# New instruction orders for an attention kernel's eight pairs, split score products in the first pair, and identity products as filler

## The chip, the cores and the metric

The kernel runs on one core of a Trainium2 chip. A core has five engines that run side by side, each through its own queue in order: TensorE (PE in the profile, its weight loads PEld), VectorE (DVE), ScalarE (ACT), GpSimd (POOL) and SyncE (SP), which here only issues transfers. They meet through semaphores. The metric is the time of one execution on the device in microseconds (us); lower is better. Of the kernel before there are three timed runs and one profiled execution.

## The reference, cut to what matters

```python
# attention: q, k, v are (2, 8, 768, 64) in float32, centroids (8, 16, 64)
q_assign = argmax(einsum(q_n, c_n), -1)         # q_n, k_n, c_n: rows divided by their norms
k_assign = argmax(einsum(k_n, c_n), -1)
mask = q_assign[:, :, :, None] == k_assign[:, :, None, :]
scores = where(mask, (1 / sqrt(D)) * q @ k.T, -1e9)
attn = softmax(scores)
x = (attn @ v) laid out as (1536, 512)
# two layers on 1536 tokens, widths 512 -> 2048 -> 512
h = x @ w1_in;  g = h * cos(h);                              x = g @ w1_out
h = x @ w2_in;  g = h, 0 or (h + 1)**2 / 4, by the size of h;  out = g @ w2_out
```

Every query attends to the keys whose nearest centroid is the same as its own. The cluster test is folded into the score product as extra rows: a second product with few contraction rows adds zero where the clusters agree and a huge negative number where they don't.

## The kernel before, in words

The attention part works on eight pairs of heads (two batches, four pairs of heads each). Each pair has twelve score tiles of 128 queries by 768 keys, `S0` to `S11`; `S0` to `S5` are its first head. A tile is four products on TensorE, two for each half of the keys: one of 128 contraction rows (line 635), and one of 96 rows in the first pair, 80 in the others, which adds the low parts and the clusters (line 638). Then VectorE takes the row maxima (line 645, called max here) and ScalarE the exponential with its row sum (line 653, called Exp here). Two score tiles fit into PSUM at a time, so tile n+2 can begin on TensorE only after Exp of tile n.

Of the first head the exponentials are turned by TensorE (`G`, three 128x128 transpositions into one bank, line 696, which ScalarE copies out, line 698) and multiplied by v (`V`, line 703); VectorE scales the sum by the softmax denominators (`X`, line 713). Of the second head VectorE turns the tile in squares of 32 (`T`, line 741) and TensorE multiplies small blocks of 32 rows (`W`, four steps, line 757); `Z` (lines 769 and 770) adds the partial sums up. `R` is the reciprocal of the row sums (ScalarE line 660, VectorE 661 and 663), `B` spreads it through DRAM. Each pair's q and k are prepared during the pair before: `L` loads, `Q0` to `Q3` turn (line 544) and are copied out, `D`, `C`, `m`, `t`, `n`, `O` find the clusters, `H` and `J` copy the rows into place by DMA.

The order of all this is written out by hand. For each pair a string of words is read from left to right (`run_cycle`), and each word emits its instructions on all engines at once: `BEGIN` for the first pair, `FIRST` for the second, `CYCLE` for the next four, `LATE` and `LAST` for the last two. A prime on a word means the pair before. Nothing is rearranged later, so each engine runs its share in just this order. `w` is one step of converting the layers' weights (mostly one VectorE instruction), `h` one early product of the first layer, `g0` the first of its cosines.

The first pair is prepared by `first_pair`, which ends with its first three tiles. While nothing else is ready there, `run_idle` multiplies a tile of zeros (line 345): `NIDLE` says how many at each of five places. `centroid_setup` loads the exponential's table on ScalarE ahead of need, by an `Exp` whose two result columns go into the tile that takes q of the second pair; so that load waits for it. The two score banks share PSUM with a pool `ps_q` that the preparation uses and closes.

After the eight pairs come the two layers: 2304 products of 128x512 on TensorE, with the element-wise work on the other engines.

Of the kernel before, what the change touches and what calls it, by code (L numbers as in the profile page):

```python
# [9 lines left out]
F32 = mybir.dt.float32  # L10
# [23 lines left out]
NIDLE = (9, 3, 2, 4, 2)  # L34
# [3 lines left out]
def attention_moe_moe(  # L38
# [214 lines left out]
    with ExitStack() as actx:  # L253
# [6 lines left out]
        idle = ap.tile([P, HS], F32, tag="pt", bufs=PT_BUFS, name="idle").bitcast(BF16)[:, :512]  # L260
# [52 lines left out]
        def centroid_setup(ct):  # L313
# [7 lines left out]
            nc.scalar.activation(nat[1][0][:, 0, 0, 0:2],  # L321
# [17 lines left out]
        def first_pair():  # L339
# [9 lines left out]
            run_idle(NIDLE[0])  # L349
# [140 lines left out]
            times(1, nc.gpsimd)  # L490
            one = Prep(1)
# [4 lines left out]
            run_idle(NIDLE[4])  # L496
# [5 lines left out]
            ps_q.close()  # L502
            ps_s.append(actx.enter_context(tc.tile_pool(name="ps_s", bufs=2, space=PSUM, reuse_waits="tile")))
            scores_of(0)
            one.turn(3)
            scores_of(1)
# [118 lines left out]
        def scores(n, step):  # L625

            d, j = divmod(n, NJ)
            i, h = divmod(d, 2)
            qt, kt = prepped[i][h]
            if step == 0:  # L630
                ptile[n] = ps_s[0].tile([P, 2, 512], F32, tag="s", name=f"s{n}")
            s = ptile[n]
            cols = slice(j * P, (j + 1) * P)
            kc = slice(step * HS, (step + 1) * HS)
            nc.tensor.matmul(s[:, step, :HS], qt[:, 0, cols], kt[:, 0, kc],  # L635
                             start=True, stop=False)
            rows = D + C if i else D + 2 * C
            nc.tensor.matmul(s[:, step, :HS], qt[:rows, 1, cols], kt[:rows, 1, kc],  # L638
                             start=False, stop=True)
# [160 lines left out]
        def run_cycle(c, order):  # L800
# [4 lines left out]
            for word in words:  # L805
# [8 lines left out]
                if not 0 <= i < NP and what not in "wIAqhg":  # L814
# [250 lines left out]
```

## Time and profile before

| what | value |
|---|---|
| timed runs | 757.41, 758.57, 761.39 us, median 758.57 |
| profiled execution | 758.55 us; its span from first to last instruction is 756.6 us |
| TensorE busy | 744.2 us of the span (98%) |
| VectorE busy | 593.4 us (78%) |
| ScalarE busy | 372.5 us (49%) |
| GpSimd busy | 266.8 us (35%) |
| mean granted TensorE clock | 0.998 |

The span is what the trace covers; the 1.95 us between the span and the time of that execution lie around it. Matmuls overlap in their pipelines, so a busy TensorE may still run slower than its best; distances from one start to the next show that better than busy time. "Idle before" in a row is the engine's idle time right ahead of it, and the arrow names what ended it. The granted clock is 1.00 at 2.4 GHz and 0.50 at 1.2 GHz.

### The profile page before, as it was taken

Reading aid. Unit: us, or ns where it says so; the run is one execution under the profiler, and the core shown is the slowest. Engines: PE = TensorE matmul, PEld = TensorE weight load, DVE = VectorE, ACT = ScalarE, POOL = GpSimd, SP = SyncE. Lnnn points to the kernel's source line nnn. Section 1 sums busy time; section 2 is a strip of 40 time slices with the busy share of each in tenths; the row PEclk is TensorE's granted clock in tenths of the full one; section 3 lists DMA queues with packets and bytes.
Section 4 is the critical chain, followed back from the end, with each engine's and each line's share of the span. In section 5 each row is a group of like instructions: output and inputs, shape, how many; then the busy total and the mean of one; then the engine's idle time right before and its main releaser. Section 6 shows DMA issues by size and latency. Waiting matters only on the chain.

```text
span 756.6 us, 13126 instructions
## 1 busy us (share of the span) xinstructions
PE 744.2 (98%) x4957; PEld 592.5 (78%) x4957; DVE 593.4 (78%) x961; ACT 372.5 (49%) x727; POOL 266.8 (35%) x415
## 2 busy tenths in 40 slices
PE   8899999999999999999999999999999999999998
PEld 5577777777677788888888888888888888888887
DVE  5779777978886999888688769978867886895552
ACT  5878677877775545734334443224434322322220
POOL 6454586574363365212122113422212221121110
PEclk9999999999999999999999999999999999999999
DMA  8959777977532233122022111212311221200012
GB/s 200 226 143 224 176 176 180 219 170 201 151 82 79 83 112 113 55 84 84 28 84 84 56 52 60 84 29 83 93 48 55 84 75 38 81 4 0 29 38 101
DMA packets 77710, 74.98 MB, mean 99 GB/s; under 512 B 29488, under 2 KB 69648, under 8 KB 77648
## 3 DMA queue, kind: packets, MB, share of 16 engines
q1 hardware_dynamic: 77360, 73.99, 36.5%
q8 instruction: 39, 0.64, 0.3%
q14 instruction: 23, 0.19, 0.1%
q10 hardware_dynamic: 288, 0.16, 0.1%
HBM read 50.89 MB, written 3.19 MB: 71 GB/s over the span
## 4 chain that ended last, share of the span: by engine, by line
PE 91%; DVE 4%; ACT 2%; DMA 1%; issue 1%; SPq 0%; DVEq 0%; ACTq 0%
PE y L941 11%; PE y L942 11%; PE y L943 11%; PE big L941 11%; PE big L942 11%; PE big L943 11%; PE s L635 5%; PE big L757 4%; PE s L638 4%; PE big L696 4%; PE big L703 4%; DVE nm L645 1%; PE big L544 1%; ACT p L653 1%; PE big L562 1%
## 5 line engine op out<-in xcount | busy, mean ns | idle before, releaser
L941 PE MATMUL big<-xh,w 128*128 128x512 f32 x368 | 143.4, 390 | 0.6 <-DVE g L920 0.6
L943 PE MATMUL big<-xh,w 128*128 128x512 f32 x368 | 143.2, 389 | 0.0
L942 PE MATMUL big<-xl,w 128*128 128x512 f32 x368 | 143.2, 389 | 0.0
L905 POOL TENSOR_SCALAR gh<-g 128x512 fp32r<-128x512 f32 x96 | 62.4, 650 | 196.9 <-DVE g L934 119.0
L645 DVE TENSOR_REDUCE nm<-s 128x1 f32<-128x768 f32 x96 | 90.4, 948 | 18.1 <-PE s L638 16.5
L191 POOL TENSOR_SCALAR w<-wx 128x512 fp32r<-128x512 f32 x64 | 45.2, 706 | 164.1 <-DVE wx L184 159.9
L930 ACT ACTIVATE p<-big,ones 128x512 f32<-128x512 f32 x48 | 33.2, 691 | 136.9 <-DVE m L929 136.9
L653 ACT ACTIVATE p<-s,nm 128x768 f32<-128x768 f32 x96 | 86.4, 904 | 22.2 <-DVE nm L645 19.9
L941 PEld LDWEIGHTS big<-xh,w 128*128 128x128 f32 x368 | 69.1, 188 | 15.7 <-DVE g L920 1.5
L943 PEld LDWEIGHTS big<-xh,w 128*128 128x128 f32 x368 | 69.1, 188 | 14.4
L942 PEld LDWEIGHTS big<-xl,w 128*128 128x128 f32 x368 | 69.1, 188 | 14.2
L635 PE MATMUL s<-st,st 128*128 128x384 f32 x192 | 73.8, 384 | 4.7 <-ACT p L653 3.6
L164 ACT ACTIVATE wx<-wraw 128x512 f32<-128x512 f32 x64 | 42.6, 666 | 68.5 <-DVE w L194 58.5
L941 PE MATMUL y<-gh,w 128*128 128x512 f32 x192 | 74.7, 389 | 0.0
L942 PE MATMUL y<-gl,w 128*128 128x512 f32 x192 | 74.7, 389 | 0.0
L943 PE MATMUL y<-gh,w 128*128 128x512 f32 x192 | 74.7, 389 | 0.0
L942 PE MATMUL y<-w,gh 128*128 128x512 f32 (+1 forms) x192 | 74.3, 387 | 0.0
L943 PE MATMUL y<-w,gl 128*128 128x512 f32 (+1 forms) x192 | 74.3, 387 | 0.0
L941 PE MATMUL y<-w,gh 128*128 128x512 f32 (+1 forms) x192 | 74.3, 387 | 0.0
L909 DVE TENSOR_TENSOR gl<-g,gh 128x512 fp32r<-128x512 f32 x94 | 65.1, 693 | 8.2 <-POOL gh L905 7.4
L1010 DVE TENSOR_TENSOR acc<-y,acc 128x512 f32<-128x512 f32 x71 | 48.3, 684 | 28.7 <-PE y L943 28.7
L638 PE MATMUL s<-st,st 80*128 80x384 f32 (+1 forms) x192 | 65.4, 341 | 0.0
(163 smaller groups left out, 1421.4 us busy)
## 6 DMA issues: line engine op xcount, KB each, us to landing
wraw<-in_moe_w_in_dram SPq DMA_DIRECT2D x32, 512.0 KB
wraw<-in_moe_w_out_dram SPq DMA_DIRECT2D x32, 512.0 KB, 3.5
vr<-in_v_dram SPq DMA_DIRECT2D x32, 192.0 KB, 4.6
st<-tt SPq DMA_DIRECT2D x31, 192.0 KB, 4.0
nat<-in_q_dram SPq DMA_DIRECT2D x8, 384.0 KB, 4.9
nat<-in_k_dram SPq DMA_DIRECT2D x8, 384.0 KB
st<-tt SPq DMA_DIRECT2D x8, 384.0 KB
st<-xh SPq DMA_DIRECT2D x8, 384.0 KB, 6.2
```

What stands on the lines that cost most here:

```text
L164: nc.scalar.activation(x, high.bitcast(F32), AF.Abs)
L191: nc.gpsimd.tensor_scalar(hi, x, 1.0, 0.0, ALU.mult, ALU.add)
L635: nc.tensor.matmul(s[:, step, :HS], qt[:, 0, cols], kt[:, 0, kc], start=True, stop=False)
L638: nc.tensor.matmul(s[:, step, :HS], qt[:rows, 1, cols], kt[:rows, 1, kc], start=False, stop=True)
L645: nc.vector.tensor_reduce(nm, s[:, :, :HS], AX.XY, ALU.max, negate=True)
L653: nc.scalar.activation(p.rearrange("p (a n) -> p a n", a=2), s[:, :, :HS], AF.Exp, bias=nm, accum_out=dens[d][:, jj:jj + 1])
L905: nc.gpsimd.tensor_scalar(hi, g, 1.0, 0.0, ALU.mult, ALU.add)
L909: side.tensor_tensor(lo, g, hi.bitcast(F32), ALU.subtract)
L941: nc.tensor.matmul(o, lh, rh, start=first, stop=False)
L942: nc.tensor.matmul(o, lh, rl, start=False, stop=False)
L943: nc.tensor.matmul(o, ll, rh, start=False, stop=last)
L1010: nc.vector.tensor_tensor(a, po, a, ALU.add)
```

## The change

In the first pair, the 128-row products of tiles 0 and 1 are emitted together, ahead of the copies of the cluster rows into place, and the 96-row products of both follow after them; the third transposition of k for the next pair comes behind both tiles. The pool of the score tiles is opened earlier for that. The advance `Exp` writes two spare columns instead of the next pair's q tile. The zero products at the very start are six of 192 columns in float32 in place of nine of 512 in bf16; the fourth idle place has five products in place of four, and the fifth has none. A new word `i` multiplies the identity by n copies of itself into a free bank (`keep_busy`). All five strings are new. `CYCLE` and `FIRST` have `Q1` ahead of `S0` instead of behind it, `Q2` and `V5'` earlier, and `n` right behind `t`. `BEGIN` has `i3` twice, `LATE` `i2`, `LAST` `i4`.

```diff
-NIDLE = (9, 3, 2, 4, 2)
+NIDLE = (6, 3, 2, 5, 2)
...
-        idle = ap.tile([P, HS], F32, tag="pt", bufs=PT_BUFS, name="idle").bitcast(BF16)[:, :512]
+        idle = ap.tile([P, HS], F32, tag="pt", bufs=PT_BUFS, name="idle")
...
-            nc.scalar.activation(nat[1][0][:, 0, 0, 0:2],
+            nc.scalar.activation(spare[:, 5:7],
                                  desc[:, 0:2], AF.Exp, scale=0.0)
...
-            run_idle(NIDLE[0])
+            for _ in range(NIDLE[0]):
+                nc.tensor.matmul(idle_o[:, :192], idle[:, :P], idle[:, :192],
+                                 start=True, stop=True)
...
             times(1, nc.gpsimd)
+            ps_q.close()
+            ps_s.append(actx.enter_context(tc.tile_pool(name="ps_s", bufs=2, space=PSUM, reuse_waits="tile")))
             one = Prep(1)
...
             po = [turn_rows(0, 1, (0,)), turn_rows(0, 1, (1,)), turn_rows(0, 0)]
-            run_idle(NIDLE[4])
+            for n in range(2):
+                for step in range(2):
+                    scores(n, step, (0,))
             put_rows(0, 1, po[0], nc.vector)
...
             one_hot(1)
-            ps_q.close()
-            ps_s.append(actx.enter_context(tc.tile_pool(name="ps_s", bufs=2, space=PSUM, reuse_waits="tile")))
-            scores_of(0)
+            for n in range(2):
+                for step in range(2):
+                    scores(n, step, (1,))
+                row_max(n)
             one.turn(3)
-            scores_of(1)
             row_exp(0)
...
+        def keep_busy(n):
+            nc.tensor.matmul(big[ring[0]][:, :n * P].rearrange("p (a n) -> p a n", a=n), ident,
+                             ident.unsqueeze(1).to_broadcast([P, n, P]), start=True, stop=True)
...
-        CYCLE = ("Q0 H0' S0 Q1 E0 S1 E1 T10' Q2 O' V5' S2 Q3 E2 T11' S3 D v' X' J0' G0 E3 S4 W0' S5 W1' J1' R1' L W2' E4 Y' E5 H1' W3' Z' S6 R0 S7 G2 G1 G3 C V0 B1' E6 m E7 T6 V1 T7 G7 G6 G5 t S8 G4 S9 G10 E8 E9 n V2 V3 r B0 G8 T8 G9 S10 G11 S11 T9 V4 E10 z' E11 ")
+        CYCLE = ("Q0 Q1 H0' S0 Q2 E0 S1 V5' E1 v' Q3 T10' S2 T11' O' E2 S3 D X' G0 E3 L R1' J0' H1' S4 W0' S5 W1' E4 W2' W3' E5 Y' Z' S6 G1 G2 R0 J1' G3 S7 B1' C G7 E6 m T6 V0 E7 V1 t n G6 G10 G5 S8 T7 G4 S9 r E8 G8 V2 B0 T8 V3 z' E9 G11 S10 G9 S11 T9 V4 E10 E11 ")
...
```

Three places in order. The first is TensorE in the first pair, from the last zero product to the next pair's cluster products; `s0` and `s1` are the score tiles, `nat1` is k of the second pair. Before:

```order
L345 MATMUL big3_87<-idle_91 128x512
L635 MATMUL s0_297<-st1_0_0_167,st0_0_0_166 128x384
L638 MATMUL s0_297<-st1_0_0_167,st0_0_0_166 128x384
L635 MATMUL s0_297<-st1_0_0_167,st0_0_0_166 128x384
L638 MATMUL s0_297<-st1_0_0_167,st0_0_0_166 128x384
L544 MATMUL big2_86<-ident_60,nat1_1_148 128x128 x3
L635 MATMUL s1_312<-st1_0_0_167,st0_0_0_166 128x384
```

And now:

```order
L643 MATMUL s0_287<-st1_0_0_164,st0_0_0_163 128x384 x2
L643 MATMUL s1_290<-st1_0_0_164,st0_0_0_163 128x384 x2
L647 MATMUL s0_287<-st1_0_0_164,st0_0_0_163 128x384 x2
L647 MATMUL s1_290<-st1_0_0_164,st0_0_0_163 128x384 x2
L551 MATMUL big2_86<-ident_60,nat1_1_145 128x128 x3
```

The four 128-row products (now line 643) stand in front, the four 96-row ones (647) behind them, and the transpositions of k, which stood between the tiles, come last.

The second place is TensorE in `BEGIN`, around tile `s5`; `p0` to `p2` are exponentials of the first tiles, `nat2` is q of the third pair. Before:

```order
L696 MATMUL big0_84<-ident_60,p0_302 128x128
L696 MATMUL big0_84<-ident_60,p1_317 128x128
L696 MATMUL big0_84<-ident_60,p2_339 128x128
L635 MATMUL s5_389<-st1_0_0_167,st0_0_0_166 128x384
L638 MATMUL s5_389<-st1_0_0_167,st0_0_0_166 128x384
L635 MATMUL s5_389<-st1_0_0_167,st0_0_0_166 128x384
L638 MATMUL s5_389<-st1_0_0_167,st0_0_0_166 128x384
L597 MATMUL big1_85<-ident_60,xh_73 128x128 x3
L544 MATMUL big2_86<-ident_60,nat2_0_397 128x128 x3
L544 MATMUL big0_84<-ident_60,nat2_0_397 128x128 x3
```

And now:

```order
L551 MATMUL big0_84<-ident_60,nat2_0_380 128x128 x3
L705 MATMUL big1_85<-ident_60,p0_301 128x128
L705 MATMUL big1_85<-ident_60,p1_306 128x128
L705 MATMUL big1_85<-ident_60,p2_335 128x128
L551 MATMUL big2_86<-ident_60,nat2_0_380 128x128 x3
L643 MATMUL s5_414<-st1_0_0_164,st0_0_0_163 128x384
L647 MATMUL s5_414<-st1_0_0_164,st0_0_0_163 128x384
L643 MATMUL s5_414<-st1_0_0_164,st0_0_0_163 128x384
L647 MATMUL s5_414<-st1_0_0_164,st0_0_0_163 128x384
L896 MATMUL big0_84<-ident_60 128x384
```

Two turns of the third pair's q moved from behind `s5` to ahead of it, and an identity product (line 896) stands behind `s5`.

The third place is the start of `LAST`. On TensorE, from the second half of tile `s87` (the last pair's `S3`) on; `p6_t` are turned exponentials of the pair before, `ptb6` its turned squares. Before:

```order
L635 MATMUL s87_3073<-st1_7_0_2252,st0_7_0_2251 128x384
L638 MATMUL s87_3073<-st1_7_0_2252,st0_7_0_2251 128x384
L703 MATMUL big3_87<-p6_t10_2916,v32_6_2732 64x384
L703 MATMUL big3_87<-p6_t11_3035,v32_6_2732 64x384
L635 MATMUL s88_3087<-st1_7_0_2252,st0_7_0_2251 128x384
L638 MATMUL s88_3087<-st1_7_0_2252,st0_7_0_2251 128x384
L635 MATMUL s88_3087<-st1_7_0_2252,st0_7_0_2251 128x384
L638 MATMUL s88_3087<-st1_7_0_2252,st0_7_0_2251 128x384
L696 MATMUL big2_86<-ident_60,p84_3049 128x128
L696 MATMUL big2_86<-ident_60,p85_3060 128x128
L696 MATMUL big2_86<-ident_60,p86_3070 128x128
L635 MATMUL s89_3101<-st1_7_0_2252,st0_7_0_2251 128x384
```

And now:

```order
L643 MATMUL s87_3074<-st1_7_0_2250,st0_7_0_2249 128x384
L647 MATMUL s87_3074<-st1_7_0_2250,st0_7_0_2249 128x384
L896 MATMUL big2_86<-ident_60 128x512
L643 MATMUL s88_3086<-st1_7_0_2250,st0_7_0_2249 128x384
L647 MATMUL s88_3086<-st1_7_0_2250,st0_7_0_2249 128x384
L643 MATMUL s88_3086<-st1_7_0_2250,st0_7_0_2249 128x384
L647 MATMUL s88_3086<-st1_7_0_2250,st0_7_0_2249 128x384
L705 MATMUL big2_86<-ident_60,p84_3048 128x128
L705 MATMUL big2_86<-ident_60,p85_3058 128x128
L705 MATMUL big2_86<-ident_60,p86_3069 128x128
L766 MATMUL big0_84<-ptb6_2926,vr6_2921 64x192 x2
L766 MATMUL big1_85<-ptb6_2926,vr6_2921 64x192 x2
```

The two products of `V5'` moved up, to between `s85` and `s86`; an identity product of 512 columns stands in their place; and the first step of `W` (now line 766) comes ahead of `s89` instead of behind it.

On VectorE at the same place, from the maxima of the last pair's first tile on (`nm84`) to those of its fifth. Before:

```order
L645 TENSOR_REDUCE nm84_3050<-s84_3044 128x1
L174 TENSOR_SCALAR wx_2739<-wx_2739 128x512
L645 TENSOR_REDUCE nm85_3061<-s85_3055 128x1
L741 STREAM_TRANSPOSE ptb6_2944<-p82_3005 128x24x32
L645 TENSOR_REDUCE nm86_3071<-s86_3065 128x1
L645 TENSOR_REDUCE nm87_3079<-s87_3073 128x1
L741 STREAM_TRANSPOSE ptb6_2944<-p83_3028 128x24x32
L713 TENSOR_TENSOR rb12_2960<-big3_87,rb12_2960 128x384
L645 TENSOR_REDUCE nm88_3093<-s88_3087 128x1
```

And now:

```order
L654 TENSOR_REDUCE nm84_3049<-s84_3043 128x1
L654 TENSOR_REDUCE nm85_3059<-s85_3053 128x1
L750 STREAM_TRANSPOSE ptb6_2926<-p82_3007 128x24x32
L654 TENSOR_REDUCE nm86_3070<-s86_3064 128x1
L174 TENSOR_SCALAR wx_2762<-wx_2762 128x512
L654 TENSOR_REDUCE nm87_3080<-s87_3074 128x1
L750 STREAM_TRANSPOSE ptb6_2926<-p83_3028 128x24x32
L722 TENSOR_TENSOR rb12_2974<-big3_87,rb12_2974 128x384
L654 TENSOR_REDUCE nm88_3092<-s88_3086 128x1
```

One step of the weights' conversion (line 174) moved from behind the first maxima to behind the third; the rest stands as before.

## Rows read from the trace of the kernel before

**Rows 1.** The page's head.

```profile
span 756.6 us, 13126 instructions
```

**Rows 2.** Engines' busy time by stage: stretch, length, busy (instructions), granted clock, DMA.

```profile
126.80:152.40 25.60, 25.60 (x333) 19.38 (x332) 20.68 (x32) 20.70 (x49) 16.09 (x25) 1.00 0.77 184
247.00:756.60 509.60, 506.37 (x2244) 419.69 (x2244) 398.45 (x647) 188.84 (x311) 126.88 (x175) 1.00 0.21 65
```

**Rows 3.** Who waited for whom on TensorE: total us, times, longest.

```profile
PE s L635 <- ACT p L653: 3.6, 5, 1.3
...
PE big L941 <- DVE g L920: 0.6, 1, 0.6
```

**Rows 4.** Timeline of the first pair: start, length, engine, instruction, count, [idle before].

```profile
1.19 4.02 PE L345 MATMUL big<-idle 128*128 128x512 bf16 x9 [1.19 <-DVE row L107]
...
4.84 0.60 SPq L275 DMA_DIRECT2D nat<-in_q_dram  x1
...
5.00 2.13 PE L380 MATMUL qk<-ident,nat 128*128 128x128 f32 x9
...
14.74 0.85 DVE L457 TENSOR_TENSOR dots<-tt,mx 128x192 f32<-128x192 f32 x1
...
15.66 1.99 DVE L645 TENSOR_REDUCE nm<-s 128x1 f32<-128x768 f32 x2
...
16.59 0.85 PE L562 MATMUL big<-t,cn 128*32 128x384 f32 x8
```

**Rows 5.** Timeline of BEGIN where TensorE waits longest.

```profile
23.38 0.90 ACT L653 ACTIVATE p<-s,nm 128x768 f32<-128x768 f32 x1 [2.40 <-DVE nm L645]
...
24.42 0.44 PE L635 MATMUL s<-st,st 128*128 128x384 f32 x1 [1.34 <-ACT p L653]
```

**Rows 6.** TensorE's timeline in a CYCLE: first products of S10, S0, S2.

```profile
116.33 0.42 PE L635 MATMUL s<-st,st 128*128 128x384 f32 x1
...
119.35 0.45 PE L635 MATMUL s<-st,st 128*128 128x384 f32 x1
...
122.75 0.45 PE L635 MATMUL s<-st,st 128*128 128x384 f32 x1
```

**Rows 7.** Timeline of the first half of LAST.

```profile
196.14 0.44 PE L635 MATMUL s<-st,st 128*128 128x384 f32 x1
...
197.16 0.96 DVE L645 TENSOR_REDUCE nm<-s 128x1 f32<-128x768 f32 x1 [0.20 <-PE s L638]
...
198.16 0.90 ACT L653 ACTIVATE p<-s,nm 128x768 f32<-128x768 f32 x1 [0.66 <-DVE nm L645]
...
199.20 0.44 PE L635 MATMUL s<-st,st 128*128 128x384 f32 x1 [1.05 <-ACT p L653]
...
199.24 0.97 DVE L741 STREAM_TRANSPOSE ptb<-p 128x768 f32<-128x768 f32 x1
...
203.17 0.52 DVE L713 TENSOR_TENSOR rb<-big,rb 128x384 f32<-128x384 f32 x1
...
204.89 0.49 ACT L698 ACTIVATE p_t<-big 128x384 f32<-128x384 f32 x1 [1.50 <-PE big L696]
...
205.06 0.42 DVE L176 TENSOR_SCALAR wx<-wx 128x512 int32<-128x512 int32 x1
...
205.58 4.30 PE L757 MATMUL big<-ptb,vr 32*64 32x192 f32 x192
...
207.64 0.29 ACT L660 ACTIVATE den<-den,ones 128x6 f32<-128x6 f32 x1
...
209.81 0.44 PE L635 MATMUL s<-st,st 128*128 128x384 f32 x1
```

**Rows 8.** Engines' busy time around the fall of TensorE's clock; columns as in rows 2.

```profile
198.20:201.62 3.42, 2.19 (x10) 1.50 (x12) 3.18 (x5) 2.36 (x5) 2.98 (x3) 1.00 1.05 237
201.62:205.03 3.41, 3.41 (x13) 2.44 (x10) 2.91 (x4) 1.70 (x5) 1.49 (x1) 0.50 0.39 125
```

**Rows 9.** Timeline of LAST's end: X of the last pair.

```profile
233.72 0.56 DVE L713 TENSOR_TENSOR rb<-big,rb 128x384 f32<-128x384 f32 x1 [0.76 <-DMA rb<-flat]
```

More of the change, by code (lines that the diff above doesn't have):

```diff
@@ L623, in attention_moe_moe, with scores @@
         NS = 2 * NJ
-        def scores(n, step):
+        def scores(n, step, parts=(0, 1)):
             d, j = divmod(n, NJ)
@@ L629, in scores @@
             qt, kt = prepped[i][h]
-            if step == 0:
+            if step == 0 and 0 in parts:
                 ptile[n] = ps_s[0].tile([P, 2, 512], F32, tag="s", name=f"s{n}")
@@ L634, in scores @@
             kc = slice(step * HS, (step + 1) * HS)
[L635 to L639, printed above, removed]
+            if 0 in parts:
+                nc.tensor.matmul(s[:, step, :HS], qt[:, 0, cols], kt[:, 0, kc],
+                                 start=True, stop=False)
+            if 1 in parts:
+                rows = D + C if i else D + 2 * C
+                nc.tensor.matmul(s[:, step, :HS], qt[:rows, 1, cols], kt[:rows, 1, kc],
+                                 start=False, stop=True)
         def row_max(n):
@@ L813, in run_cycle @@
                     i += 1
-                if not 0 <= i < NP and what not in "wIAqhg":
+                if not 0 <= i < NP and what not in "wIAqhgi":
                     continue
@@ L880, in run_cycle @@
                     first_h(min(ahead[0] + 1, 36))
+                elif what == "i":
+                    keep_busy(arg)
                 elif what == "w":
                     pump(arg or 1)
-        BEGIN = ("m' S3 E3 G0 t' S4 G2 G4 E4 n' S5 L' E5 O' Q0 Q1 H0' S6 S7 Q2 G5 G1 E6 G3 E7 Q3 G8 H1' T6 L J0' V0 G7 S8 S9 G6 R0 E8 T7 V1 r E9 D T8 J1' G10 V2 V3 C T9 m G9 B0 G11 S10 S11 E10 t E11 n V4 ")
-        FIRST = ("Q0 H0' S0 Q1 E0 S1 E1 T10' Q2 O' V5' S2 Q3 E2 T11' S3 D v' X' J0' G0 E3 S4 W0' S5 W1' J1' R1' L W2' E4 Y' E5 H1' W3' Z' S6 R0 S7 G2 G1 G3 C V0 B1' E6 m E7 T6 V1 T7 G7 G6 G5 t S8 G4 S9 G10 E8 E9 n V2 V3 r B0 G8 T8 G9 S10 G11 S11 T9 V4 E10 z' E11 ")
@@ new lines, in attention_moe_moe @@
+        BEGIN = ("m' S3 i3 G2 S4 G0 t' n' E3 L' Q0 G4 H0' E4 Q1 S5 i3 S6 E5 O' H1' G1 E6 S7 R0 G3 Q2 V0 T6 E7 S8 G6 Q3 S9 T7 G8 J0' G5 V1 D E8 V2 B0 G7 C L m E9 S10 T8 J1' G11 T9 V3 r t G9 G10 S11 V4 E10 n E11 ")
+        FIRST = ("Q0 Q1 H0' S0 Q2 E0 S1 V5' E1 v' Q3 T10' S2 T11' O' E2 S3 D X' G0 E3 L R1' J0' H1' S4 W0' S5 W1' E4 W2' W3' E5 Y' Z' S6 G1 G2 R0 J1' G3 S7 B1' C G7 E6 m T6 V0 E7 V1 t n G6 G10 G5 S8 T7 G4 S9 r E8 G8 V2 B0 T8 V3 z' E9 G11 S10 G9 S11 T9 V4 E10 E11 ")
+        CYCLE = ("Q0 Q1 H0' S0 Q2 E0 S1 V5' E1 v' Q3 T10' S2 T11' O' E2 S3 D X' G0 E3 L R1' J0' H1' S4 W0' S5 W1' E4 W2' W3' E5 Y' Z' S6 G1 G2 R0 J1' G3 S7 B1' C G7 E6 m T6 V0 E7 V1 t n G6 G10 G5 S8 T7 G4 S9 r E8 G8 V2 B0 T8 V3 z' E9 G11 S10 G9 S11 T9 V4 E10 E11 ")
@@ new lines, in attention_moe_moe @@
+        LATE = ("S0 I0 I2 V5' E0 T10' S1 E1 X' S2 T11' O' I1 i2 S3 J0' E2 G0 E3 Y' v' H0' S4 W0' w S5 W1' w W2' W3' A0 R1' E4 H1' w E5 w Z' w R0 S6 G10 G1 E6 S7 E7 r T6 G3 V0 G6 S8 T7 G2 G4 w G9 E8 S9 B0 V1 w w G5 G11 w G8 w S10 J1' V2 E9 T8 G7 S11 E10 E11 B1' V3 z' V4 T9 ")
+        LAST = ("S0 E0 S1 V5' T10' S2 w E1 S3 T11' E2 X' i4 S4 E3 w R1' G0 E4 W0' v' B1' Y' w S5 W1' W2' W3' E5 w Z' w S6 G5 E6 h h S7 G3 G2 T6 S8 E7 G6 G1 h E8 T7 r S9 h h T8 G7 E9 h G4 T9 S10 h S11 V0 E10 V1 E11 w z' R0 V2 h V3 T10 q R1 G8 h h G9 T11 G10 w B0 w G11 W0 B1 h g0 W1 W2 w W3 V4 h Z w V5 X z k Y ")
```

5 lines of the change are left out of this document (2 added, 3 removed).

## The prediction

> **What bounds the kernel now.** I read the busy time by stage first. In a middle stretch of one CYCLE's length TensorE is busy for all of its 25.60 us, and in the two layers for 506.37 of 509.60, while VectorE and ScalarE stand at about 80% in the CYCLE [rows 2]. So TensorE sets the pace there, and an order can only move its work about: the number of products in a CYCLE is the same before and after. Next I read the list of waits on TensorE, to see what there is to win. The largest item is 3.6 us, in five waits of a score tile's first product (line 635) for an exponential (line 653): two score banks, so tile n+2 waits for Exp of tile n. Behind it come 0.6 us in which the first layer waits for its cosine's VectorE step [rows 3]. The timeline says where these lie. The longest of the five, 1.34 us, ends at 24.42 in BEGIN [rows 5], and one of 1.05 us ends at 199.20 in LAST [rows 7]. Last I read the granted clock: after the waits in LAST it stood at 0.50 from 201.62 to 205.03, and at 1.00 again behind that; in the 3.42 us ahead of the fall TensorE was busy for 2.19 [rows 8]. At most half of those 3.41 us, 1.7, is what the slow clock can cost. So the attention has some 3.6 + 0.6 + 1.7 = 5.9 us that another order could win, out of 756.6 [rows 1].
>
> How long is the loop through a score bank? From the first product to the maxima 1.02 (196.14 to 197.16), to Exp 1.00 (198.16), to the next tile in that bank 1.04 (199.20), so 3.06 us [rows 7]. A tile stalls when less work than this lies between the starts of tiles n and n+2, or when VectorE or ScalarE come late.
>
> **The start: +0.1.** The zero products lasted from 1.19 to the first transposition at 5.00, nine of 0.43 at half clock [rows 4]. No row has a float32 product of 128x128 by 192 columns. From below: a transposition of 128 columns takes 0.21 here ((2.13 - 0.42) / 8, with 0.42 the last one's length, an estimate), so 192 columns 0.32, and six 1.9 us. From above: the cluster products of line 562, four side by side of 384 columns in eight records of 0.85 us in all [rows 4], take no more than 0.85 at full clock; half the columns at half the clock is 0.85 again, and six are 5.1. I take 0.65 each, 3.9 in all: the near row is that of the products, and its 0.85 holds the way through the array once, which six in a row don't pay each. So the transpositions start about 0.1 later than 5.00, the larger tile of zeros included. With the low end they would wait for the loads instead. Ends: -0.5 to +1.3.
>
> The Trainium skill, page "FP8 and Floating Point Precision", section "TensorE Precision Notes", says that true float32 takes four passes through the array. By that, an estimate: 192 columns four times at 1.2 GHz are 0.64 us, six of them 3.84, and the start would move by nothing; a product of 384 columns at full clock is 0.64. The row of line 562 agrees with it for products (0.85 with the way through the array); the transpositions at 5.00, also float32, take half of that [rows 4]. By the page the identity products cost twice what transpositions of the same width cost.
>
> **The second pair's load: 0.** It was issued at 4.84, after the advance Exp [rows 4]; now it goes out right behind the first pair's load. That takes it out of the way of the copies that fill `st`, which tile S0 needs. But what is late next? VectorE: it runs line 457 from 14.74 to 15.59, and then the maxima of S0 and S1 from 15.66 to 17.65 without a gap [rows 4]. Tiles that stand ready sooner wait for it. Upside if the chain in front of VectorE moves as well: -1.0.
>
> **The split tiles: 0.** Eight products of tiles 0 and 1 are the same eight. The 128-row ones can now run before the cluster rows are copied into place, while VectorE does those copies. The maxima stay where VectorE lets them, at 15.7. The cost is on the other side: k's third transposition now comes behind both tiles, so its copy, the cluster products at 16.59 [rows 4] and tile S2 behind them may be late by the length of half a tile; this is covered as long as the tiles start earlier by as much. Ends: -0.4 to +0.4.
>
> **BEGIN: 0.** Its wait of 1.34 us before S5 came from Exp of S3, which itself waited 2.40 for the maxima [rows 5]: VectorE has the cluster rows and `m` in front of them. That order of VectorE is the same now. TensorE gets two turns of q (Q0, Q1) into the wait, six transpositions at 0.11, so 0.6 us of useful work; but ScalarE now has the copies of two `G` banks in front of Exp of S3, and those of Q0 and G4 in front of Exp of S4. Each is about 0.49 [rows 7], and one of them comes after ScalarE had been idle anyway. So I let S5 and S6 come 0.3 later each and set both against the 0.6. The identity products `i3`, 0.33 (three transpositions) to 0.85 each, stand in the remaining wait; if that is gone they cost all of it. Ends: -1.3 to +1.3.
>
> **The cycles: 0.** From S10 to the next S0 there are 3.02 us, from S0 to S2 3.40 (116.33, 119.35, 122.75) [rows 6]. With Q1 moved to ahead of S0, 0.36 go from the second to the first: 3.38 and 3.04. The shortest distance is 3.0 before and after, about the loop's 3.06, and in the stretch of rows 2 it left TensorE without idle time. So five cycles cost nothing; what hides the loop is the same slack in another place. The end if it isn't hidden is a rival below.
>
> **LATE: 0.** `i2` is 0.22 to 0.6 and stands between S2 and S3, where tiles wait for Exp. Nothing else is added; the order of `w`, `A0` and the exponentials has S4's Exp behind the first conversion step, with the weights' load long issued. Ends: -1.0 to +0.5.
>
> **LAST: -0.3.** I count from S0's start. Before, S6 starts at 209.81 - 196.14 = 13.67 [rows 7]. Now: maxima of S0 at 1.0, of S1 at 1.95, T10' (0.97) until 3.9; S2 at 3.06, its maxima 4.1 to 5.0; then `w` (0.4), maxima of S3 to 6.35, T11' to 7.3, X' (0.52) to 7.85. ScalarE: Exp of S3 to 7.4, then R1' (0.29) to 7.7, and the copy of G0 (0.49) to 8.2. The first step of W writes the bank of that copy, so it starts at 8.2. Four steps take 4.30 together [rows 7] and S5 in their midst 0.7, so W ends and S6 starts at about 13.3. TensorE gains a W step ahead of S5, and loses nearly all of it to the wait for that copy. The identity product of 512 columns (0.43 to 1.1) stands between S3 (4.0) and S4 (6.1), covered. Whether the clock falls again is open; TensorE has `i4` and `V5'` spread over the waits now, so I leave it at 1.00, which the count assumes. Ends: -1.7 to +0.9.
>
> **The end of the attention: -0.8.** X of the last pair waited 0.76 us for its denominators' DMA, at 233.72 [rows 9]. `B0` stood behind `B1` and is now in front of the first W. VectorE then gets X and all behind it up to 0.76 sooner, and the first layer's cosines, on which TensorE waited 0.6 [rows 3], come in time. I take 0.6 for that wait and 0.2 for smaller ones between tiles. Ends: -1.4 to +0.3.
>
> **Sum.** +0.1 - 0.3 - 0.8 = -1.0. The profiled execution took 758.55 us (756.6 of span [rows 1] and 1.95 around it), and the median of the timed runs is 758.57; so 757.5.
>
> **Rivals.** *The waits are really filled.* For it speaks that all five sit where the new strings put work, and that the identity products stand next to each. Against it: VectorE and ScalarE, which cause them, have the same work in nearly the same order. Then the 3.6 of the waits and the 1.7 of the clock go, some 0.9 comes back as filler on the path [rows 3, 8]: -4.4, 754.1.
>
> *The cycles stall.* With 3.04 from S0 to S2 and T10', T11' between the maxima, VectorE has three maxima, and a transposition of 0.97, between S0 and Exp of S2; where it is late, S2 and S3 wait. It decides if VectorE enters a cycle more than 0.1 us late. Price: the 0.36 that moved, once or twice in each of five cycles, 1.8 to 3.6; on 757.5 this is 759.3 to 761.1, say 760.2, slower than before. Against it: the end of the cycle got the same 0.36 as slack, and before it had the tight place.
>
> *The orders only move the waits.* Identity products and moved turns fill time in which TensorE waited, and the waits, whose cause is VectorE's and ScalarE's order, stay: 758.5.
>
> **Chances.** Forecast 0.48, filled waits 0.22, stalled cycles 0.15, only moved 0.15. The forecast's own range is 755.9 to 759.1, from the ends above taken not all at once. The range for 8 in 10 reaches to the other cases, 754.0 to 760.6. A measurement of this kernel can tell about 0.5% (3.8 us) from no change, so faster means under 754.8 and slower over 762.4: faster 0.20 (most of the filled waits and a bit of the forecast), slower 0.07 (the worse end of the stalled cycles and what I don't see), same 0.73.
>
> **What would show it.** Right: cycles of 25.6 us, S5 of BEGIN within half a microsecond of 24.4, the maxima of S0 at about 15.7, S6 of LAST 13.3 us after S0, and no wait on the cosine at the first layer. Wrong: a granted clock of 0.50 anywhere behind the start, a wait for Exp in each cycle, zero products that end well before 5.0, or tiles of the first pair whose maxima come a microsecond sooner.

## The result, and the profile after

The changed kernel takes 767.80 us (median of 767.48, 767.74, 767.86 and 769.37); the kernel before, timed beside it, 758.35. The ratio is 1.0123, 95% interval [1.0094, 1.0153]. So it is 9.4 us slower, where 757.5 had been forecast and 760.6 was the upper end. The span went from 756.6 [rows 1] to 766.0 us. The lines of the tiles stand 8 or 9 higher in the changed kernel: the score products are L643 and L647, max L654, Exp L662, the transpositions of `G` L705, `X` L722, `W` L766.

The first thing to make is a table of where the time went, from the start of each pair's S0 to that of the next:

| stretch | before | after | difference |
|---|---|---|---|
| start to S0 | 14.68 | 14.43 | -0.25 |
| BEGIN | 26.42 | 27.00 | +0.58 |
| FIRST | 25.65 | 26.11 | +0.46 |
| four CYCLEs | 26.98, 25.62, 25.58, 25.62 | 26.76, 27.58, 26.94, 27.08 | +4.56 |
| LATE | 25.59 | 30.16 | +4.57 |
| S0 of LAST to the end | 560.46 | 559.90 | -0.56 |

Half of the loss is in LATE, half is spread over the cycles, and both ends gained. TensorE's waits answer to [rows 3] (total us, times, longest):

```profile
PE s L643 <- ACT p L662: 3.9, 9, 0.8
PE big L705 <- ACT p L662: 3.5, 1, 3.5
PE big L766 <- issue: 1.3, 2, 1.0
...
PE big L956 <- DVE g L935: 0.3, 1, 0.3
```

The five waits of a score tile for Exp have become nine, and there is a new one of 3.5 us. The busy time by stage answers to [rows 2, 8]: one CYCLE's stretch, LATE just after the long wait, and the layers.

```profile
121.88:147.48 25.60, 24.77 (x321) 18.38 (x321) 19.35 (x30) 19.49 (x47) 16.55 (x25) 1.00 0.80 182
186.17:189.58 3.41, 3.41 (x53) 2.35 (x52) 1.39 (x2) 3.15 (x8) 1.20 (x2) 0.50 1.03 249
...
256.80:766.00 509.20, 505.93 (x2244) 419.50 (x2242) 398.46 (x647) 188.90 (x311) 126.20 (x175) 1.00 0.20 65
```

TensorE is no longer busy all through a CYCLE, and behind the wait in LATE its clock was at 0.50 for 3.41 us. LAST, where it fell before, kept 1.00.

**LATE.** The timeline of the changed kernel, from the transfers to TensorE:

```profile
175.18 1.96 SPq L302 DMA_DIRECT2D vr<-in_v_dram  x4
...
177.24 2.08 SPq L691 DMA_DIRECT2D rb<-flat  x2
...
182.91 0.56 DVE L722 TENSOR_TENSOR rb<-big,rb 128x384 f32<-128x384 f32 x1 [3.32 <-DMA rb<-flat]
183.38 0.95 DVE L654 TENSOR_REDUCE nm<-s 128x1 f32<-128x768 f32 x1
...
184.36 0.90 ACT L662 ACTIVATE p<-s,nm 128x768 f32<-128x768 f32 x1 [3.12 <-DVE nm L654]
...
185.41 0.33 PE L705 MATMUL big<-ident,p 128*128 128x128 f32 x1 [3.47 <-ACT p L662]
```

`X'` needs the denominators' broadcast, which SyncE issued at 177.24, behind four loads of v's rows. `X'` now stands in front of the maxima of S2, so VectorE waits 3.32 us with the maxima queued behind it; Exp, the first transposition and S4 follow.

**The cycles.** What grew is no single wait on TensorE. It shows on the queues that issue transfers. SyncE's list of waits over pairs 3 to 6 has one row in the changed kernel that the list of before has not (total us, times, longest):

```profile
SPq L678 <- POOL line L675: 15.2, 4, 5.4
```

At L678 SyncE writes the line of denominators (`R1'`) to DRAM. GpSimd must have written the line first, and everything else that SyncE issues is queued behind. Followed on SyncE and GpSimd from one such write to the next, the kernel before shows this (write, broadcast of `B1'`, `z'` on GpSimd, line, next write):

```profile
132.14 0.42 SPq L669 DMA_DIRECT2D flat<-line  x1
...
140.72 0.89 SPq L677 DMA_DIRECT2D rb<-flat  x1
...
144.70 1.83 POOL L775 TENSOR_TENSOR xs<-xs,rb 64x768 f32<-64x768 f32 x1 [6.34 <-DMA rb<-flat]
...
156.07 1.05 POOL L666 TENSOR_SCALAR line<-turned 6x32 f32<-6x32 f32 x4 [0.31 <-DVE turned L663]
...
157.18 0.42 SPq L669 DMA_DIRECT2D flat<-line  x1
```

and the changed kernel this:

```profile
135.66 0.28 SPq L678 DMA_DIRECT2D flat<-line  x1
...
147.75 0.59 SPq L686 DMA_DIRECT2D rb<-flat  x1
...
151.26 1.82 POOL L784 TENSOR_TENSOR xs<-xs,rb 64x768 f32<-64x768 f32 x1 [9.62 <-DMA rb<-flat]
...
162.26 1.05 POOL L675 TENSOR_SCALAR line<-turned 6x32 f32<-6x32 f32 x4
...
163.33 0.29 SPq L678 DMA_DIRECT2D flat<-line  x1
```

It is a loop through two in-order queues: the write lets the broadcast go, the broadcast lets `z'` run on GpSimd, behind `z'` stand the roundings of the next q and k and the next line, and SyncE waits for that line. Before, it took 8.58 + 3.98 + 11.37 + 1.11 = 25.04 us, and GpSimd still waited 0.31 for VectorE ahead of the line, so others set the pace. After, it takes 12.09 + 3.51 + 11.00 + 1.07 = 27.67 and GpSimd waits for nothing between `z'` and the line. The two rounds ahead of these are alike: 25.19 and 26.16 us before, with waits of 0.39 and 0.88 for VectorE, and 26.95 and 27.57 after, with none. The first leg grew by 3.5: the copies of the one-hot rows (`J0'`, `J1'`, eight of them) went out ahead of the write, and now go out behind it, ahead of the broadcast (the two loads of `L` moved the other way). The loop is longer than TensorE's 25.6 us. Time in which TensorE waited for nothing that the profile shows ("issue") is no rival: 1.3 us in the four CYCLEs, 0.9 before. The steps behind it come late in turn: `n` waits for GpSimd (0.3 to 1.4 us a cycle), S10 and S11 for Exp, and LATE's broadcast is issued 1.3 us after S0 of LATE, where before it was issued 4.5 us ahead of it (166.09 for 170.55).

### The profile page after: what moved, and what is told of

Read it like the earlier page. It is cut to its first block, busy times and chain, and to the rows that moved or that the text cites. A ratio compares the mean times of both kernels' runs of the same rounds, so it can differ in the third digit from the quotient of the medians.

```text
span 766.0 us, 13136 instructions
## 1 busy us (share of the span) xinstructions
PE 748.8 (98%) x4966; PEld 594.9 (78%) x4967; DVE 594.8 (78%) x961; ACT 372.0 (49%) x727; POOL 266.5 (35%) x415
## 4 chain that ended last, share of the span: by engine, by line
PE 86%; DVE 5%; ACT 3%; DMA 3%; POOL 2%; issue 1%; SPq 1%; DVEq 0%; POOLq 0%; ACTq 0%
PE y L957 11%; PE y L956 11%; PE y L958 11%; PE big L956 11%; PE big L957 11%; PE big L958 11%; PE s L643 4%; PE big L766 4%; PE s L647 3%; PE big L705 3%; PE big L712 3%; ACT p L662 1%; DVE nm L654 1%; DMA nat<-in_k_dram 1%; PE big L551 1%
## 5 line engine op out<-in xcount | busy, mean ns | idle before, releaser
L662 ACT ACTIVATE p<-s,nm 128x768 f32<-128x768 f32 x96 | 86.4, 901 | 34.0 <-DVE nm L654 33.5
L654 DVE TENSOR_REDUCE nm<-s 128x1 f32<-128x768 f32 x96 | 90.1, 943 | 13.8 <-PE s L647 12.5
L643 PE MATMUL s<-st,st 128*128 128x384 f32 x192 | 73.5, 385 | 5.2 <-ACT p L662 3.9
L647 PE MATMUL s<-st,st 80*128 80x384 f32 (+1 forms) x192 | 64.9, 341 | 0.0
```

The source lines that it names most:

```text
L654: nc.vector.tensor_reduce(nm, s[:, :, :HS], AX.XY, ALU.max, negate=True)
L662: nc.scalar.activation(p.rearrange("p (a n) -> p a n", a=2), s[:, :, :HS], AF.Exp, bias=nm, accum_out=dens[d][:, jj:jj + 1])
```

## The experiments

Eighteen kernels, each timed over five rounds beside the kernel before (whose medians in these sittings were 758.2 to 759.1).

| run | what it is | median us | ratio to before |
|---|---|---|---|
| late_x_back | changed, X' back in LATE | 764.31 | 1.0089 [1.0061, 1.0117] |
| loads_behind | changed, the sixth pair's loads behind the broadcast | 764.32 | 1.0103 [1.0082, 1.0124] |
| cyc_n_back | changed, n back | 769.05 | 1.0136 [1.0119, 1.0152] |
| four_back | changed, n, G, Q1, X' back | 763.68 | 1.0085 [1.0070, 1.0101] |
| old_cycles | changed, old FIRST, CYCLE, LATE | 759.42 | 1.0009 [0.9997, 1.0022] |
| load_early | old_cycles, L of BEGIN earlier | 758.80 | 1.0012 [1.0001, 1.0023] |
| no_identity | old_cycles without i3, i3, i4 | 759.09 | 1.0029 [1.0011, 1.0046] |
| only_start | before, new first pair and BEGIN | 759.62 | 1.0021 [1.0003, 1.0039] |
| only_last | before, new LAST | 758.84 | 1.0009 [0.9996, 1.0022] |
| new_head | before, first half of the new cycle | 765.22 | 1.0095 [1.0074, 1.0116] |
| new_tail | before, second half | 759.04 | 1.0018 [1.0000, 1.0037] |
| new_tail_n | new_tail, n and G back | 765.46 | 1.0088 [1.0059, 1.0116] |
| head_r | new_head, R1' back | 762.71 | 1.0053 [1.0034, 1.0072] |
| after_r | changed, R1' back | 776.59 | 1.0231 [1.0209, 1.0253] |
| after_r_x | after_r, X' back | 777.21 | 1.0250 [1.0227, 1.0272] |
| before_r | before, R1' ahead | 775.63 | 1.0218 [1.0196, 1.0240] |
| head_transfers_old | new_head, five words of transfers back | 758.24 | 0.9992 [0.9978, 1.0006] |
| after_transfers_old | changed, the five words and X' back | 762.50 | 1.0038 [1.0021, 1.0055] |

**LATE: two runs.**

```diff
 LATE = ("S0 I0 I2 V5' E0 T10' S1 E1
-X'
 S2 T11' O' I1 i2 S3 J0' E2 G0
+X'
 E3 ...
```

> The changed kernel with one step moved: in LATE the step X' (line 722) stands behind the first bank of transpositions again, and not ahead of the maxima of tile S2. Theory (VectorE waits at X' for the denominators' DMA and holds the maxima of S2, Exp of S2 and so TensorE; the slow clock behind it is a consequence): the wait of 3.32 us at line 722 and the one of 3.47 us at line 705 go, the granted clock stays at 1.00, LATE falls from 30.16 to about 25.9 us, the time from 767.8 to 763.5. Rival (LATE is longer because of its whole new order, the place of X' only shows it): X' waits less, but another wait takes its place; LATE stays over 28.5 us, 766 to 768.

LATE fell from 30.16 to 25.83 us, at a clock of 1.00, and the median by 3.5 us (in the profiled execution another pair took 29.81, with a fall of the clock of its own). The place of `X'` and the wait that it brings are the cause, not the rest of the order.

```diff
 CYCLE of the sixth pair: "... S9
-r
 E8 G8 V2 B0
+r
 T8 ..."
```

> The changed kernel with one thing moved in the sixth pair's CYCLE alone: the four loads of v's rows (step r, line 302) are issued behind the two broadcasts of the denominators (B0, line 691), not in front of them; X' of LATE stays ahead of the maxima of S2. Theory (X' waits for the landing of that broadcast, which SP issues 2.0 us late because of the four loads): the broadcast is issued about 2 us earlier, the wait at line 722 falls from 3.3 to 1.0 to 1.5 us and the one at line 705 from 3.5 to 1.0 to 1.5, the slow clock may stay away; 764.5 to 766. Rival (the broadcast lands late since the loads and it share the DMA engines, whichever is issued first): the wait stays over 2.5 us, 767 to 768.

The same 3.5 us come back without moving `X'`, by the order of the transfers alone. In its timeline the broadcast goes out ahead of the loads, and `X'` waits 0.41 us where it waited 3.32 (this execution, the longest of six with 769.03, lost time further on in LATE, where TensorE waited 2.62 us for VectorE's partial sums):

```profile
175.61 1.18 SPq L691 DMA_DIRECT2D rb<-flat  x2
...
176.83 2.99 SPq L302 DMA_DIRECT2D vr<-in_v_dram  x4
...
180.44 0.56 DVE L722 TENSOR_TENSOR rb<-big,rb 128x384 f32<-128x384 f32 x1 [0.41 <-DMA rb<-flat]
```

So `X'` costs because two things meet: it was put early on VectorE, and its data come late on SyncE.

**My first theory of the cycles, which fell.** I saw the waits of S10 and S11 and took their neighbours for the cause: `n` right behind `t`.

```diff
 FIRST, CYCLE = ("... V1 t
-n
 G6 G10 G5 S8 T7 G4 S9 r E8
+n
 G8 V2 ...
```

> The changed kernel with one step moved: in FIRST and CYCLE the step n stands behind Exp of S8 again, as before the change, and not right behind t. Theory (VectorE waits at n, line 596, 0.3 to 1.4 us for GpSimd's product of step t and holds the maxima of S8 and S9 behind it, so that S10 and S11 wait for Exp): the waits at line 596 go, the waits of S10 and S11 for Exp in FIRST and CYCLE fall from 0.3 to 1.0 us to under 0.2, each cycle is 0.6 to 0.9 us shorter, 764.0 to 764.8. Rival (the cycles lose by the split of q's turns, with Q1 ahead of S0, or by the instruction fetches): the cycles stay at 26.1 to 27.6 us, 767 to 768.

The waits of S10 and S11 went, as expected, and no time came back. S0 of the next pair comes about 0.2 us late in their place, and in the profiled execution TensorE waited 2.00 us in FIRST for q of the fourth pair, whose load the new BEGIN issues 5 us later.

```diff
 FIRST, CYCLE = ("Q0
-Q1
 H0' S0
+Q1
 Q2 ... S6
-G1 G2
 R0 J1'
-G3
 S7
+G1 G2 G3
 B1' ...      (and n and X' as above)
```

> The changed kernel with four steps moved back: in FIRST and CYCLE n behind Exp of S8, the banks G1 and G2 behind S7 (not between S6 and S7), Q1 behind S0; in LATE X' behind G0. Theory (the loss of the changed kernel is these four places and nothing else): n gives 0.3 to 0.4 us a cycle, G behind S7 0.36 in three of them, Q1 0.2, X' 3.5 in LATE; cycles of 25.6 to 25.8 us where no instruction fetch stalls TensorE, 759.5 to 761 in all. Rival (the cycles lose as much by the order of the V and E steps at their end, z' ahead of E9 and G11 ahead of S10): S10 and S11 still wait for Exp, cycles over 26.3 us, 762 to 764.

Beyond `X'` this gave 0.6 us. S10 and S11 no longer wait, but S0 comes about 0.5 us late in every cycle, and `W` waits up to 0.5 us for `X'`. Moving the waiting steps moved the wait. SyncE's wait for GpSimd's line was still there, 17.0 us in cyc_n_back and 15.9 in four_back.

**Which part loses.** Whole strings, or halves of them:

```diff
old_cycles:
-FIRST, CYCLE, LATE = (the new ones)
+FIRST, CYCLE, LATE = (those of the kernel before)
only_start: LAST too
```

> The changed kernel with FIRST, CYCLE and LATE as before the change; the first pair, BEGIN and LAST are new. If the three strings alone made it slower: pair lengths of about 25.6 us again from the second pair to the seventh, 757 to 759. If the new start or the new LAST loses too, as the tile times of the changed kernel suggest for BEGIN (+0.6) but not for LAST (-0.5): 758 to 760. If the loss is spread over everything by something common to all of them, such as instruction fetches or where tiles lie: over 761.

> The kernel before with the new first pair, its zero products and advance Exp, and the new BEGIN; FIRST, CYCLE, LATE and LAST are as before. By the tile times of the changed kernel S0 of BEGIN comes 0.25 us sooner and S0 of FIRST 0.34 later: 758.5 to 759.2. If a head start of the first pair is worth something once the cycles behind it are the old ones: 757.8 to 758.3. If the new start shifts VectorE against TensorE so that each cycle behind it stalls: 760 to 762.

The three strings hold 8.4 of the 9.4 us (767.80 - 759.42). The new start alone is 0.2% slower, at the edge of what the runs tell, and no faster. Of the start, the trace showed one risk, the later load:

```diff
 BEGIN = ("... V0 T6
+L
 E7 S8 ... G7 C
-L
 m E9 ...
```

> The kernel of the run old_cycles (new first pair, BEGIN and LAST; FIRST, CYCLE and LATE as before the change) with one step of BEGIN moved: the load of the fourth pair's q and k (L, line 275) goes out before tile S8, as before the change, and not behind S9. Theory (the load goes out 5.0 us later in the new BEGIN, at 35.9 for 30.9, and in some executions Q0 of FIRST has to wait for it, as it did for 2.0 us in the run cyc_n_back; that is what spreads the times of old_cycles from 758.1 to 761.4): median 758.0 to 758.6, the spread under 2 us. Rival (the load's place costs nothing with the old FIRST; the spread has another cause): 759.0 to 759.8, spread as before.

Median 0.6 us lower than old_cycles, 757.2 to 760.0 for 758.1 to 761.4. But each set against the kernel before beside it, they stand at 1.0012 and 1.0009, so no gain is shown.

```diff
-BEGIN = ("m' S3 i3 G2 ... S5 i3 S6 ..."),  LAST = ("... X' i4 S4 ...")
+BEGIN = ("m' S3 G2 ... S5 S6 ..."),  LAST = ("... X' S4 ...")
```

> The kernel of the run old_cycles without the identity products of BEGIN (i3 twice) and LAST (i4); the results don't use them. Theory one (i4 keeps the clock up in LAST): the granted clock falls to 0.50 for some 3 us in LAST again, as it did before the change, S6 there comes 1 to 1.7 us later, 760.4 to 761. Theory two (the clock stays up because V5', T10' and the steps of W are spread otherwise, and the identity products only fill waits): clock 1.00, 759.0 to 759.8, the same within 0.4.

The medians agree within 0.4 us; against the kernel before beside each, the ratios are 1.0029 and 1.0009, with intervals that overlap. The mean granted clock was 0.999 or 1.000 in all twelve executions of old_cycles, and 0.993 to 0.996 in three of these twelve. That points to the identity products as what keeps the clock up now and then. It isn't shown: the trace here is of an execution at 1.000, so where the clock fell in the three is not on record, and a fourth, the longest with 762.58, had 1.000. In nine of twelve the clock stayed up without them.

```diff
 kernel before:
-LAST = (the old one)
+LAST = (the new one, with its i4)
```

> The kernel before with the new LAST alone, its identity product included. The stretch from S0 of LAST to the end was 560.46 us before and 559.94 to 560.2 in kernels with the new LAST, and the clock stayed at 1.00 there: 757.4 to 758.0, clock 1.00 in nearly all runs. If the gain in LAST is lost again by the first layer, whose cosine's wait was 0.3 to 0.8 in these runs: 758.0 to 758.6.

758.84, no gain. From S0 of LAST to the end the traces with the new LAST take 559.7 to 560.7 us, those with the old one 560.2 to 561.6, so what it wins is too little to be seen in the time. The mean granted clock was still 0.996 to 0.998 in eight of twelve executions; in the profiled one it fell in LATE, and not in LAST.

```diff
 new_head: (Q0 Q1 H0' ... Y' J1' Z' of the new string) + (S6 ... E11 of the old one)
 new_tail: (Q0 H0' ... Z' of the old string) + (S6 ... E11 of the new one)
 new_tail_n: new_tail, S6 R0 S7 G1 G2 G3 and E8 n G8
```

> The kernel before with the first half of the new FIRST and CYCLE alone (everything up to Z': Q1 ahead of S0, V5' and T10' in their new places, the load L, R1', J0', H1' ahead of S4); from S6 on the old order. Theory (the cycles lose in their second half, through n behind t, G1 and G2 between S6 and S7, and E9 late): 757.5 to 759, cycles of 25.6 to 25.8 us where no fetch stalls TensorE. Rival (the first half costs too, through the load L 2 to 3 us earlier, in the way of the instruction fetches and of the denominators' broadcast, on which X' and W wait, and through Q1): 0.3 to 0.8 us a cycle, 760 to 762.

> The kernel before with the second half of the new FIRST and CYCLE alone (from S6 on). Theory (the cycles lose in their second half): waits of S10 and S11 for Exp of 0.3 to 1.0 us each, a wait of 0.3 to 1.4 us at n for GpSimd in each cycle, G behind S6 waiting 0.3 for VectorE; cycles of 26.1 to 26.7 us, 761 to 763. Rival (the first half is it): 757.5 to 759.

> The run new_tail with two steps moved back: n behind Exp of S8, G1 and G2 behind S7. If these two are what the second half loses: cycles of 25.6 to 25.8 us, 758 to 759. If the late Exp of S9 and the bank G9 between S10 and S11 cost as well, in that S0 of the next cycle waits for Exp of S10, as it did for 0.53 us in the run four_back: cycles of 26.0 to 26.2 us, 760 to 761.5.

My theory fell here. The first half, in which hardly a tile waits for Exp, costs 6.9 us; the second, with all the waits that I had looked at, 0.7; and with its two suspects put back it costs 7.1: S0 comes about 0.5 us late in each cycle, and the mean granted clock was 0.989 to 0.995 in five of six executions. That is another loss than the loop's, for SyncE waits only 0.7 us for the line there, and no run takes it apart. In new_head SyncE waits for GpSimd's line as in the changed kernel, 17.0 us in four waits:

```profile
SPq L669 <- POOL line L666: 17.0, 4, 6.2
```

The late transfers cost most in LATE, whose string is the old one in this kernel. In the profiled execution (767.07, the longest of six) 5.0 of the 8.4 us that the span grew by lie there (30.63 us). SyncE issued the load of v 9.7 us after S0 of LATE, for 6.0 before, TensorE waited for it, and its granted clock was 0.79 from 194 to 200 us:

```profile
183.75 2.16 SPq L291 DMA_DIRECT2D v<-in_v_dram  x1
...
193.42 1.55 PE L703 MATMUL big<-p_t,v 128*64 128x384 f32 x4 [2.31 <-DMA v<-in_v_dram]
```

**The transfers.** First `R1'` alone (head_r in new_head, after_r in the changed kernel, after_r_x with `X'` back as well):

```diff
 FIRST, CYCLE = ("... G0 E3 L
-R1'
 J0' H1' S4 W0' S5 W1'
+R1'
 E4 W2' ...
```

> The run new_head (the kernel before with the first half of the new FIRST and CYCLE) with R1' alone moved back to behind W1', that is behind J0' and H1' on SyncE's queue. Theory (SyncE waits 2.9 to 3.6 us a cycle at the write of the denominators' line for GpSimd, and what is queued behind it goes out late): that wait falls under 1 us, the fetch stalls and X' waits in W shrink, LATE loses its late load of v, 758.5 to 760.5. Rival (the load L, H1' or Q1 ahead of their old places are it): 763 to 766, as new_head with 765.2.

> The changed kernel with R1' alone moved back in FIRST and CYCLE, behind W1'. Theory: SyncE's wait at line 678 falls under 1 us, z' on GpSimd starts 2 us sooner in the cycle, the waits of n for GpSimd and those of S10 and S11 for Exp shrink, the broadcast for LATE's X' goes out 2 to 3 us sooner, so that X' waits 0.5 to 1.5 us there and not 3.3; 762 to 764.5. Rival (R1' is not it): 767 to 768.

> The changed kernel with R1' back behind W1' in FIRST and CYCLE, and X' back behind G0 in LATE. If these two places are what the change loses: 758.5 to 760. If the second half of the new cycle costs by itself as well, as four_back (763.7) left open: 761 to 763.

In the first half alone it gave back 2.5 of 6.9 us, and LATE took 25.57 us again. In the changed kernel it made things worse by 8.8, and that I had not foreseen. Its waits between 66 and 200 us say why:

```profile
DVE mx L596 <- POOL tt L592: 16.2, 5, 7.7
...
PE s L643 <- ACT p L662: 13.1, 8, 6.7
...
POOL line L675 <- DMA flat<-line: 10.1, 3, 4.7
```

The line has one buffer. With the write of `R1'` behind `H1'` on SyncE, GpSimd can't write the line of `R0` until that write has landed (8.1 us once, in FIRST):

```profile
64.93 1.01 POOL L675 TENSOR_SCALAR line<-turned 6x32 f32<-6x32 f32 x4 [8.06 <-DMA flat<-line]
```

Behind `R0` on GpSimd stands `t`, on VectorE `n` waits for `t` and holds the maxima, and a tile waits 6.7 us. FIRST alone took 35.23 us, for 26.11 in the changed kernel. Next the opposite, into the old order:

```diff
 FIRST, CYCLE = ("... v' X'
+R1'
 J0' G0 E3 S4 W0' S5 W1' J1'
-R1'
 L W2' ...
```

> The kernel before with R1' alone moved ahead in FIRST and CYCLE, to in front of J0', so that SyncE writes the denominators' line ahead of the eight small copies of the one-hot rows. Theory (a write on SyncE's queue that waits for GpSimd holds all transfers behind it): SyncE waits 3 us or more a cycle at line 669, the cycles grow to 26.2 to 27.5 us, 761 to 766. Rival (the transfers have slack enough, the loss needs the other moves too): 758 to 759.5.

17 us slower, far over the range. This is the loop by itself: `J0'`, `J1'`, L and `H1'` all stand between the write and the broadcast, and nothing else differs from the kernel before. From one write to the next it takes 30.7 to 31.6 us. Part of the 17 us is a slower clock: its mean was 0.982 to 0.991, and 0.995 to 1.000 in the kernel before beside it. SyncE's list from 66 to 176 us:

```profile
SPq L669 <- POOL line L666: 25.1, 4, 7.5
```

Last, all five words that issue transfers or lead to them, in their old order, with everything else of the first half new:

```diff
 FIRST, CYCLE = ("Q0 Q1 H0' S0 Q2 E0 S1 V5' ... S3 D X'
+J0'
 G0 E3
-L R1' J0' H1'
 S4 W0' S5 W1'
+J1' R1' L
 E4 W2' W3' E5 Y'
-J1'
+H1'
 Z' S6 ...
```

> The run new_head with the five words of transfers (J0', J1', R1', L, H1') in their old order and places; SyncE's and GpSimd's queues then hold the same rows in the same order as before the change, while Q1, Q2, V5', T10', v' and the exponentials stay in their new places. Theory (the first half loses by the order of transfers): 758.3 to 759.5, z' on GpSimd at the start of a cycle again and not 1.7 us into it. Rival (the turns of q, V5' and T10' cost too, as the prediction's stalled cycles had it with 0.36 a cycle): 760 to 762.

758.24, and the wait at L669 is down from 17.0 to 0.3 us in SyncE's list. The 6.9 us of the first half are the order of these five words, and Q1, V5', T10' and `v'` in their new places cost nothing. It is the only kernel whose median is below that of before; the interval says the same speed.

> The changed kernel with the same five words back in FIRST and CYCLE, and X' behind G0 in LATE; the first pair, BEGIN, the second half of the cycles with n behind t, the rest of LATE and LAST are new. If the two places, order of transfers and X', hold the whole loss: 758.5 to 760.5 (new_tail alone had 759.0, old_cycles 759.4). If the second half, with n behind t, loses as well once it stands behind the new first half: 761 to 764.

762.5, in the second of the two ranges: 5.3 us are back, 3.4 are not. Of what is back `X'` alone gives 3.5 (late_x_back), so in the changed kernel the five words are worth 1.8 us by the medians, or 2.4 with each run set against the kernel before beside it (764.31 - 758.48 and 762.50 - 759.12). The wait at L678 for the line is down from 15.2 to 0.5 us, so the loop isn't what is left. The profiled execution has it at two places. At the end of BEGIN (28.92 us) Q0 comes 1.9 us late, waiting for q, the later load again; and in FIRST and the first CYCLE S10 and S11 wait for Exp, up to 1.0 us, with `n` waiting up to 2.0 for `t`. I have no run that takes these two away as well, so their share is read from one trace and not shown.

## Why the prediction was wrong

- *The cycles: 0.* This is the step that failed. The working counted only TensorE: the shortest distance between two tiles that share a bank, 3.0 us, which stayed the same. That part held (head_transfers_old has the 0.36 moved and is not slower). It said nothing of `L`, `R1'`, `J0'`, `J1'` and `H1'`, which the strings move too, although each issues transfers on SyncE's queue, and `R1'` puts work on GpSimd that SyncE waits for. The DMA share of 0.77 stood in the row that I used for TensorE [rows 2]. Measured: 0.46 in FIRST and 4.56 in the CYCLEs. The order of the transfers is the whole loss of the first half by itself (6.9 us, part of it in LATE); in the changed kernel putting it back gives some 2 us, and what else its cycles lose, in the second half and by the later load, stays open.
- *LATE: 0, "nothing else is added".* Wrong by 4.57. `X'` went from behind S3, E2 and G0 to ahead of S2, and its data came late because the cycle's transfers did. For the end of LAST I had read that `X` can wait for its transfer [rows 9], and didn't ask it here.
- *The stalled cycles*, the rival at 760.2, had the sign and half the size (1.8 to 3.6 for 5.0), by the wrong mechanism (Q1).
- *The start: +0.1.* The transpositions start at 5.29 for 5.00 [rows 4], the six zero products take 4.14 us in all for the 3.9 taken. The first maxima come at 15.77, where 15.7 was forecast, but not for the reason given, so that is luck: VectorE was through with line 460 at 15.17, 0.42 sooner than before, and then stood idle for 0.60 until TensorE's 96-row products were there. *The split tiles: 0* had the 128-row products run before the cluster rows are copied into place. They began at 14.43, when the last copy (line 483) had just ended; what held them, no run shows. The timeline of the first pair:

```profile
1.32 4.14 PE L351 MATMUL big<-idle 128*128 128x192 f32 x12 [1.32 <-DVE row L107]
...
5.29 1.44 PE L383 MATMUL qk<-ident,nat 128*128 128x128 f32 x9
...
13.93 0.48 ACT L483 ACTIVATE st<-big 32x384 fp32r<-32x384 f32 x1 [0.32 <-DVE st L481]
...
14.32 0.85 DVE L460 TENSOR_TENSOR dots<-tt,mx 128x192 f32<-128x192 f32 x1
...
14.43 0.94 PE L643 MATMUL s<-st,st 128*128 128x384 f32 x4 [1.19 <-DVE mx L459]
...
15.21 0.87 PE L647 MATMUL s<-st,st 96*128 96x384 f32 x4
...
15.77 1.82 DVE L654 TENSOR_REDUCE nm<-s 128x1 f32<-128x768 f32 x2 [0.60 <-PE s L647]
```

- *BEGIN: 0.* S5 at 24.87 for 24.42 [rows 5], the pair 0.58 longer, inside the bounds. What I missed is the load of the fourth pair 5 us later (35.93 for 30.91), which is a risk for FIRST.
- *LAST: -0.3, the end: -0.8.* S6 came 13.22 us after S0 (219.28 - 206.06; forecast 13.3, before 13.67 [rows 7]), W's first step waited for the copy of G0 until 7.98 after S0 (forecast 8.2), the clock stayed at 1.00, the cosine's wait fell from 0.6 to 0.3. Together -0.56 for -1.1. Right in mechanism, half in size.

## What to carry to other kernels

When an order is rewritten, list per word what it puts on every queue, those that only issue transfers included, and follow each loop that goes through them (write, broadcast, use, next write). If such a loop is as long as the stage it repeats in, it is a bound beside the busiest engine, even while its engines look idle. The engine that waits in the list shows where a loop is felt and not where it was lengthened; cut the change in halves before repairing the places that wait.

## What the runs showed of the hardware

- Without any change in a cycle's code, single executions had cycles of 25.57 to 26.93 us (only_last, whose FIRST and CYCLEs are those of before), so a cycle's length from one trace is good to about 1 us, and medians decide.
- Inside `W`, TensorE stood still for 0.99 us at 107.43 with nothing waited for ("issue"), and for 0.2 to 1.4 us at such places in most other traces. The Trainium skill, page "Runtime: NRT & Kernel Launch", section "Instruction fetch mechanics", has the engine fetch its code in blocks ahead of need, mostly hidden. One packet of the queue for instructions is on record here between 103.0 and 108.5, while the load of q and k fills the DMA engines, so these waits may be fetches that other transfers hold up; no run settles it.
- An identity product of 384 columns took 0.91 us once and 0.81 once, each in two records, one of 512 columns 1.02, at full clock; I had bounded them by 0.33 to 0.85 and 0.43 to 1.1.
